# Attention and two mixture layers on one core: where half A's weight parts are loaded, clamped and scaled, and how late the other conversions may stand

## The chip, the cores and the metric

One Trainium2 chip, one core. The metric is the device time of one execution in microseconds (us), the median of the runs shown; lower is better.

## What is computed

Inputs are q, k, v of shape 4 x 8 x 576 x 64 (batch, heads, tokens, width), a threshold tau, and two pairs of float32 weights of 512 x 2048 and 2048 x 512.

```
scores = q @ k^T / 8                            per batch and head
keep   = scores >= max(scores) - tau            else -1e9
attn   = exp(scores - max) / (sum + 1e-9)
x      = attn @ v                               as 2304 x 512
x      = g(x @ w1_in) @ w1_out                  g(h) = h * clip(h + 3, 0, 6) / 6
out    = f(x @ w2_in) @ w2_out                  f(h) = h - tanh(h)
```

The matrix products are made to float32 quality: each operand is split into a high and a low part, and three products (high x high, high x low, low x high) are summed.

## The kernel before

**Order of the work.** The kernel doesn't issue instructions as it is written. It records tasks (`add`, with an engine, an estimated duration, a key, the buffers it reads and writes, and a `slack`), and `Plan.issue` then emits them engine by engine: an engine that is free takes the ready task with the lowest key. `slack` delays the moment at which a task's successors count as ready, so it only moves instructions in each engine's order. On the chip each engine runs its instructions strictly in that order and waits on semaphores. The engines are PE (matmul), DVE, ACT, POOL (GpSimd) and SP, whose queue issues nearly all DMAs.

**Attention.** There are four batches, two column groups each, four pairs of heads. A unit is 128 rows of queries of one head (144 units; `softmax`, L561 on): PE makes 128 x 576 scores in PSUM (L577), DVE takes the maximum (L582), ACT the exponential (L584) and the threshold (L587), DVE masks (L593), ACT and POOL split the result into two float16 parts (L598, L602), and SP transposes it by a DMA (L605) for the products with v (L628). Two PSUM buffers hold scores. Per pair of heads k is transposed and split once (`k_round`, L460 to L485), `LK` units ahead of its first use; v is scaled by a power of two and split (`v_round`: sum of magnitudes on ACT L525, sum over partitions on PE L527, the power on DVE L531 to L536, scaling in place on ACT L539, high part on ACT L541, low part on POOL L543), `LV` units ahead.

**Layer 1, half A.** The hidden width of 2048 is cut in two halves, A and B. For half A layer 1 runs inside the attention stage: after each (batch, group) its tokens go through `layer1` (m tiles L388, gates L691 to L701, second product L734). Half B (`hidden`, `second`) follows after attention, then layer 2 with both halves.

**Weight conversion.** `load_w` (L334) turns a 128-wide part of a weight into a high and a low part, because the values have to pass a bit-level rounding. For each part: a DMA of 512 KB (L350 or L355) into `st`; ACT takes the magnitude of the words (L358); DVE clamps it to a range (L361, the first entry of `steps`), shifts (L363), puts the sign in (L366) and the low bits (L369); ACT writes the high part (L376); POOL subtracts for the low part (L378). There are 16 parts (8 `i`, 8 `o`) for each of: half A and half B of layer 1, half A and half B of layer 2. The working tile is `wu` (SBUF, ring `R_wu` of two); half A of layer 1 passes `scratch=R_m` and works in a PSUM buffer `m` instead, one of the two that `layer1` uses too. The ring `R_st` of three holds the loaded words.

**What sets the places.** Half A's parts are recorded one per unit with the key `T0 + STEP * (W0 + WS * n + ...)` and `slack=ST` (4.0) on the load. `weights(...)` records half B's and layer 2's: `WB` (half B, spacing `WBS`), `Ws[0]` (layer 2, half A, spread over all of half B's stage) and `Ws[1]` (layer 2, half B, from `key - W2B` with spacing `W2S`, while layer 2's first blocks run). In layer 2's first two blocks the gate's low part is on POOL (`low="pool"`, L701), so POOL works there for the gate and for the conversion.

## Time and profile before

| | us |
|---|---|
| median of 3 runs | 1147.84 |
| lowest and highest run | 1145.71, 1150.57 |
| the profiled execution, its own time | 1146.78 |
| its span, first to last instruction | 1144.7 |
| PE busy | 1073.2 (94%) |
| DVE busy | 718.4 (63%) |
| ACT busy | 616.5 (54%) |
| POOL busy | 419.0 (37%) |

The profile is read by stage, not by these averages: the attention stage with half A runs to about 515 us, half B to about 720 us, layer 2 to the end. The 2.1 us between the profiled time and the span lie before the first and after the last instruction.

### The profile page before, as it was taken

To read this page: it belongs to the slowest core of one execution; us is meant where nothing else is said; L and a number is where in the kernel's file an instruction comes from. 1 tells how busy PE (TensorE), PEld (TensorE's weight loads), DVE (VectorE), ACT (ScalarE), POOL (GpSimd) and SP (SyncE) were. 2 spreads that over 40 slices of the span, in tenths; PEclk is the share of its full clock that TensorE was granted. 3 is DMA by queue.
4 is the path that set the end of the run, shared out by engine and by line. 5 is a ranking of instruction groups with operands and counts; after the bars stand their busy time and mean duration, and the time that the engine had idled before them with its cause. 6 is when DMAs were issued, how large, how long until landed. Compare 5 with 4: busy or idle time off the path is not lost.

```text
span 1144.7 us, 23228 instructions
## 1 busy us (share of the span) xinstructions
PE 1073.2 (94%) x9104; PEld 1002.1 (88%) x9104; DVE 718.4 (63%) x1365; ACT 616.5 (54%) x1268; POOL 419.0 (37%) x420
## 2 busy tenths in 40 slices
PE   5668899999999999889999999989999999999998
PEld 4557788998999899889999999978999999999997
DVE  6889887678777867587865663995323333333232
ACT  6868888689677867445544443544323323323222
POOL 3666767667656765652412210465200000000000
PEclk8668899999999999999999999999999999999999
DMA  7889678777977787778633430241100000000000
GB/s 186 180 190 230 131 183 156 173 148 188 164 168 144 167 155 129 210 198 282 184 93 94 129 94 1 76 131 33 38 1 19 1 19 19 1 19 20 1 20 19
DMA packets 257454, 125.77 MB, mean 110 GB/s; under 512 B 200257, under 2 KB 250945, under 8 KB 257345
## 3 DMA queue, kind: packets, MB, share of 16 engines
q1 hardware_dynamic: 247296, 114.72, 43.0%
q0 software_dynamic: 9504, 9.44, 3.6%
q8 instruction: 72, 1.18, 0.4%
q14 instruction: 38, 0.30, 0.1%
q10 hardware_dynamic: 544, 0.13, 0.1%
HBM read 62.92 MB, written 18.87 MB: 71 GB/s over the span
## 4 chain that ended last, share of the span: by engine, by line
PE 74%; DVE 8%; issue 5%; ACT 5%; POOL 3%; DMA 3%; SPq 0%; POOLq 0%; DVEq 0%; ACTq 0%
PE ya L388 24%; PE m L388 18%; PE h L388 12%; PE s L577 7%; PE m L734 6%; PE tp L628 5%; DVE e L593 2%; PE tp L460 2%; POOL bi L378 1%; DVE z L582 1%; ACT e L584 1%; POOL g L701 1%; DMA pt<-pp 1%; DMA st<-in_moe_w_in_dram 1%; DVE st L369 1%
## 5 line engine op out<-in xcount | busy, mean ns | idle before, releaser
L602 POOL TENSOR_TENSOR pp<-e,pp 128x128 f16<-128x128 f32 (+3 forms) x160 | 185.4, 1179 | 119.3 <-ACT pp L598 58.3
L698 ACT ACTIVATE g<-t 128x256 fp32r<-128x256 f32 x216 | 90.0, 417 | 103.8 <-DVE t L905 78.2
L582 DVE TENSOR_REDUCE z<-s 128x1 f32<-128x576 f32 x144 | 108.2, 753 | 53.3 <-PE s L577 52.4
L701 DVE TENSOR_TENSOR g<-t,g 128x256 fp32r<-128x256 f32 x184 | 92.9, 505 | 71.9 <-PE ya L388 44.6
L593 DVE SCALAR_TENSOR_TENSOR e<-s,z,e 128x576 f32<-128x576 f32 x144 | 116.1, 811 | 15.6 <-ACT e L584 9.9
L388 PE MATMUL m<-xT,ai 128*128 128x256 f32 (+1 forms) x768 | 121.7, 304 | 3.7 <-DVE t L693 2.5
L577 PE MATMUL s<-ks,q 128*128 128x288 f32 x512 | 105.2, 334 | 17.2 <-DVE e L593 16.5
L388 PE MATMUL ya<-ao,g 128*128 128x512 f32 x432 | 113.7, 396 | 5.8 <-POOL g L701 4.8
L388 PE MATMUL ya<-g,bo 128*128 128x256 f32 x864 | 116.1, 283 | 2.0 <-DVE g L701 1.9
L584 ACT ACTIVATE e<-s,z 128x576 f32<-128x576 f32 x144 | 105.4, 738 | 23.3 <-DVE z L582 18.3
L388 PE MATMUL h<-x,bi 128*128 128x256 f32 x864 | 115.4, 283 | 0.1
L388 PE MATMUL m<-x,bi 128*128 128x256 f32 x864 | 115.1, 283 | 0.0
L388 PEld LDWEIGHTS h<-x,bi 128*128 128x128 f32 x864 | 111.0, 191 | 3.3 <-POOL bi L378 0.3
L388 PEld LDWEIGHTS m<-x,bi 128*128 128x128 f32 x864 | 111.0, 191 | 3.0
L388 PEld LDWEIGHTS m<-xT,ai 128*128 128x128 f32 x768 | 107.9, 192 | 6.0 <-DVE t L693 3.5
L388 PEld LDWEIGHTS ya<-g,bo 128*128 128x128 f32 x864 | 108.9, 192 | 2.8 <-DVE g L701 2.5
L388 PE MATMUL ya<-bo,g 128*128 128x512 f32 x432 | 111.2, 393 | 0.0
L577 PEld LDWEIGHTS s<-ks,q 128*128 128x128 f32 x512 | 81.7, 210 | 24.4 <-issue 9.3
L628 PE MATMUL tp<-vt,pt 128*128 128x65 f16 (+1 forms) x2240 | 87.9, 199 | 8.1 <-DMA pt<-pp 4.5
L388 PEld LDWEIGHTS ya<-ao,g 128*128 128x128 f32 x432 | 75.9, 189 | 21.1 <-POOL g L701 7.8
L628 PEld LDWEIGHTS <-pt 128*128 128x128 f16 (+1 forms) x2240 | 79.7, 104 | 16.3 <-DMA pt<-pp 6.5
L905 DVE TENSOR_TENSOR t<-h,t 128x256 f32<-128x256 f32 x72 | 30.4, 423 | 98.8 <-ACT t L903 98.8
(101 smaller groups left out, 1825.2 us busy)
## 6 DMA issues: line engine op xcount, KB each, us to landing
st<-in_moe_w_in_dram SPq DMA_DIRECT2D x32, 512.0 KB, 3.9
st<-in_moe_w_out_dram SPq DMA_DIRECT2D x32, 512.0 KB, 4.0
x<-xs POOLq DMA_DIRECT2D x18, 512.0 KB, 5.4
xs<-xT SPq DMA_DIRECT2D x8, 640.0 KB, 4.8
y<-ys SPq DMA_DIRECT2D x9, 512.0 KB, 8.9
kr<-in_k_dram SPq DMA_DIRECT2D x16, 256.0 KB, 3.1
vr<-in_v_dram SPq DMA_DIRECT2D x16, 256.0 KB, 3.6
xs<-xT SPq DMA_DIRECT2D x8, 512.0 KB, 4.5
```

What stands on the lines that cost most here:

```text
L388: nc.tensor.matmul(ps, l[a], r[b], start=first and t == 0 and i == 0, stop=last and t == 2 and i == n - 1,)
L460: nc.tensor.transpose(ps[:, o:o + w], s.rearrange("p r d -> p (r d)"), ident[p0:p0 + w, p0:p0 + w])
L577: nc.tensor.matmul(ps.t[:, half, 0:SH], l, ks[:, half * SH:(half + 1) * SH], start=i == 0, stop=i == len(ops) - 1,)
L582: add("dve", 0.69, key, lambda: nc.vector.tensor_reduce(out=z.t[:, 0:1], in_=s(), axis=AX.XY, op=ALU.max, negate=True), r=[ps], w=[z])
L584: exp = add("act", 0.66, key, lambda: nc.scalar.activation(out=ex(), in_=s(), func=ACTF.Exp, bias=z.t[:, 0:1]), r=[ps, z], w=[e])
L593: add("dve", 0.74, key, lambda: nc.vector.scalar_tensor_tensor(out=ex(), in0=s(), scalar=z.t[:, 1:2], in1=ex(), op0=ALU.is_ge, op1=ALU.mul ...
L602: add("pool", t_pool(w * (src.stop - src.start)), key, lambda src=src, dst=dst: nc.gpsimd.tensor_tensor(out=pp.t[:, 0:w, dst], in0=e.t[:, ...
L628: nc.tensor.matmul(pv.t[0:m, w_ * (D + 1):(w_ + 1) * (D + 1)], pt.t[:, n, blk, rows], vv, start=o == 0, stop=o == len(ops) - 1)
L698: hi = add("act", t_act(n, sbuf=True), key, lambda: nc.scalar.activation(out=gh(), in_=t(), func=ACTF.Copy), r=[bt], w=[bh])
L701: add(low, t_pool(n) if low == "pool" else t_dve(n), key, lambda: eng.tensor_tensor(out=gl(), in0=t(), in1=gh().bitcast(F32), op=ALU.subtr ...
L734: prev = [add("pe", t_mm(n, 1), kd, lambda p=p, l=l, r=r, m=m, s=s, ps=ps: nc.tensor.matmul(ps.t[:, 0:n], W["o", m].t[:, l, s], r[m].t[:, ...
L905: add("dve", t_dve(n), key, lambda: nc.vector.tensor_tensor(out=s_(), in0=p(), in1=s_(), op=ALU.subtract), r=[ps, t], w=[t])
```

## The change

Five things are changed, by numbers of the planner and in `load_w` and `v_round`:

- The first two weight parts of half A are loaded on ACT's queue at the start, with no slack (`queue=n < 2`); the later ones stay on SP's.
- k's first round stands one unit later (`LK` 5 to 4), and the first batch's v rounds stand three units later (`u + 2` for the first pairs in place of `u - LV`).
- v is scaled on POOL in place of ACT.
- In half A's conversion the magnitude is written to `wu` in SBUF, the clamp works there, and only the shift moves on to the PSUM buffer; the first four parts' clamps (`NCL = 4`) are on POOL, the other twelve on DVE. Half B's and layer 2's conversions keep their tile and engine.
- Slacks: `cs` of 0.1 (half B), 0.3 and 0.2 (layer 2) on the tasks of a conversion, three times that on the magnitude; the spacing of layer 2's half B goes from 3.0 to 4.0 (`W2S`).

```diff
-    LK, LQ, LV, LD = 5, 3, 1, 4
+    LK, LQ, LV, LD = 4, 3, 1, 4
+    CB, CC, CD = 0.1, 0.3, 0.2
-    W2B, W2S = 6.0, 3.0
+    W2B, W2S = 6.0, 4.0
+    NCL = 4
...
-        wst, wu, W = R_st.new(), (scratch or R_wu).new(), R_w[name, kind, m].new()
+        wst, wu, W = R_st.new(), R_wu.new(), R_w[name, kind, m].new()
+        sc = scratch.new() if scratch else wu
+        mid = lambda dt: sc.t.bitcast(dt)
+        eng, sync = ("act", nc.scalar) if queue else ("dma", nc.sync)
...
+        def clamp():
+            (nc.gpsimd if low else nc.vector).tensor_scalar(
+                out=part(F32), in0=part(F32), scalar1=TINY, scalar2=HUGE, op0=ALU.max, op1=ALU.min)
...
-            out=part(F32), in_=raw(1).bitcast(F32), func=ACTF.Abs), r=[wst], w=[wu], slack=cs)
+            out=part(F32), in_=raw(1).bitcast(F32), func=ACTF.Abs), r=[wst], w=[wu], slack=3 * cs)
+        if low:
+            add("pool", t_pool(DM), key + 3, clamp, r=[wu], w=[wu], slack=cs)
+        else:
+            add("dve", 0.5, key + 3, clamp, r=[wu], w=[wu], slack=cs)
         steps = [
-            lambda: nc.vector.tensor_scalar(
-                out=part(F32), in0=part(F32), scalar1=TINY, scalar2=HUGE, op0=ALU.max, op1=ALU.min),
             lambda: nc.vector.tensor_scalar(
-                out=part(I32), in0=part(I32), scalar1=3, scalar2=0x3FFFFFF8,
+                out=mid(I32), in0=part(I32), scalar1=3, scalar2=0x3FFFFFF8,
...
-        add("act", t_act(N, sbuf=True, scalars=True), key, lambda: nc.scalar.activation(
-            out=raw(), in_=raw(), func=ACTF.Copy, scale=sv.t[:, 2 * j:2 * j + 1]), r=[vr, sv], w=[vr])
+        add("pool", t_pool(N), key, lambda: nc.gpsimd.tensor_scalar(
+            out=raw(), in0=raw(), scalar1=sv.t[:, 2 * j:2 * j + 1], scalar2=None, op0=ALU.mult), r=[vr, sv], w=[vr])
...
-                rounds.append((u - LV, ("v", b, j)))
+                rounds.append((u + 2 if u < 4 else u - LV, ("v", b, j)))
...
-                    "a", kind, m, ..., 0.8, slack=ST, scratch=R_m, cs=CS)
+                    "a", kind, m, ..., 0.8, slack=ST if n > 1 else 0.0, scratch=R_m, cs=CS, queue=n < 2, low=n < NCL)
```

Line numbers of the changed kernel are 11 higher behind `load_w`; in it the magnitude is L367, the clamp L363, the shift L374.

How the order moves, at three places. First ACT's first instructions (ks: k's split, q: q's split, vt and vr: v, st: loaded words, wu: magnitude, e: exponential). Before:

```order
L449 DMA qr<-in_q_dram 128x2x64 x2
L483 ACT_TABLE_LOAD
L483 ACTIVATE ks<-tp 64x2x256 x2
L490 ACTIVATE q<-tp,tau_b 128x512
L525 ACTIVATE vt_94,vs<-vr 128x10x64
L483 ACTIVATE ks<-tp 64x2x64 x2
L539 ACTIVATE vr<-vr,sv 128x640
L483 ACTIVATE ks<-tp 64x2x256 x2
L541 ACTIVATE vt_94<-vr 128x10x64
L584 ACTIVATE e<-s,z 128x576
```

And with the change:

```order
L460 DMA qr<-in_q_dram 128x2x64 x2
L355 DMA st<-in_moe_w_in_dram 128x4x256 x2
L494 ACT_TABLE_LOAD
L494 ACTIVATE ks<-tp 64x2x256 x2
L501 ACTIVATE q<-tp,tau_b 128x512
L494 ACTIVATE ks<-tp 64x2x64
L367 ACTIVATE wu<-st 128x512
L494 ACTIVATE ks<-tp 64x2x64
L494 ACTIVATE ks<-tp 64x2x256 x2
L595 ACTIVATE e<-s,z 128x576
```

Two weight loads stand ahead of ACT's table load, a magnitude stands where v's first sum stood, and two passes over v are gone from ahead of the first exponential.

Second, DVE at the last masked unit of attention (z: maximum and threshold, e: mask, wu: half B's conversion). Before:

```order
L582 TENSOR_REDUCE z<-s 128x1
L590 TENSOR_SCALAR z<-z,tau_b 128x1
L361 TENSOR_SCALAR wu<-wu 128x512
L363 TENSOR_SCALAR wu<-wu 128x512
L593 SCALAR_TENSOR_TENSOR e<-s,z,e 128x576
L366 SCALAR_TENSOR_TENSOR wu<-st,wu 128x512
```

With the change:

```order
L593 TENSOR_REDUCE z<-s 128x1
L601 TENSOR_SCALAR z<-z,tau_b 128x1
L604 SCALAR_TENSOR_TENSOR e<-s,z,e 128x576
L363 TENSOR_SCALAR wu<-wu 128x512
L374 TENSOR_SCALAR wu<-wu 128x512
```

The last mask now stands ahead of half B's first clamp and shift, no longer behind them.

Third, POOL where layer 2's half B (bi, bo) is converted among the gates' low parts (g); the end of that stretch, of 32 g in all. Before:

```order
L378 TENSOR_TENSOR bi_11357<-st,bi_11357 128x512
L701 TENSOR_TENSOR g<-t,g 128x256
L378 TENSOR_TENSOR bo_11406<-st,bo_11406 128x512
L701 TENSOR_TENSOR g<-t,g 128x256 x2
L378 TENSOR_TENSOR bi_11443<-st,bi_11443 128x512
L701 TENSOR_TENSOR g<-t,g 128x256
L378 TENSOR_TENSOR bo_11475<-st,bo_11475 128x512
L701 TENSOR_TENSOR g<-t,g 128x256 x14
```

With the change:

```order
L389 TENSOR_TENSOR bi_11423<-st,bi_11423 128x512
L712 TENSOR_TENSOR g<-t,g 128x256 x2
L389 TENSOR_TENSOR bo_11475<-st,bo_11475 128x512
L712 TENSOR_TENSOR g<-t,g 128x256
L389 TENSOR_TENSOR bi_11518<-st,bi_11518 128x512
L712 TENSOR_TENSOR g<-t,g 128x256 x2
L389 TENSOR_TENSOR bo_11566<-st,bo_11566 128x512
L712 TENSOR_TENSOR g<-t,g 128x256 x11
```

The 16 parts stood among the first 18 gates and stand among the first 21.

## Rows read from the trace of the kernel before

**Rows 1.** Windows by stage: length, PE, PEld, DVE, ACT, POOL busy us, PE clock, DMA, GB/s.

```profile
7.30:20.00 12.70, 7.38 (x32) 5.96 (x32) 8.80 (x16) 9.45 (x20) 2.09 (x3) 0.91 0.93 254
20.00:96.60 76.60, 53.29 (x431) 44.93 (x431) 68.93 (x116) 59.31 (x113) 50.03 (x45) 0.64 0.86 187
96.60:136.00 39.40, 31.80 (x373) 28.98 (x370) 37.64 (x66) 35.17 (x77) 28.21 (x29) 0.91 0.77 157
136.00:461.00 325.00, 315.57 (x3584) 300.36 (x3582) 247.87 (x484) 254.28 (x487) 212.53 (x216) 0.99 0.80 164
720.00:790.00 70.00, 64.19 (x414) 56.56 (x413) 62.36 (x91) 34.70 (x75) 42.13 (x37) 1.00 0.31 98
```

**Rows 2.** Waits of PE from 0 to 140 us: total us, times, longest us.

```profile
PE s L577 <- DVE e L593: 18.7, 14, 4.9
```

**Rows 3.** DVE's maximum to 130 us: busy us, mean ns, idle before it, releaser.

```profile
L582 DVE TENSOR_REDUCE z<-s 128x1 f32<-128x576 f32 x35 | 26.2, 751 | 5.5 <-PE s L577 5.3
```

**Rows 4.** The clamp's line: lowest, median, highest ns, first and last start.

```profile
L361 DVE TENSOR_SCALAR wu<-wu x48: 408/426/2416, 462.0 to 780.7; 128x512 f32<-128x512 f32 x48
L361 DVE TENSOR_SCALAR m<-m x16: 681/690/700, 23.2 to 127.2; 128x512 f32<-128x512 f32 x16
```

**Rows 5.** POOL's groups to 130 us, columns as in rows 3.

```profile
L602 POOL TENSOR_TENSOR pp<-e,pp 128x1024 f16<-128x1024 f32 x15 | 32.1, 2138 | 0.0
L378 POOL TENSOR_TENSOR ai<-st,ai 128x512 fp32r<-128x512 f32 x8 | 10.4, 1300 | 4.3 <-ACT ai L376 4.3
L543 POOL TENSOR_TENSOR vt<-vr,vt 128x640 f16<-128x640 f32 x4 | 5.4, 1357 | 5.9 <-ACT vt L541 5.9
L453 POOL COPY qr<-qr 128x256 f32<-128x256 f32 x10 | 4.0, 400 | 6.8 <-DMA qr<-in_q_dram 6.8
```

**Rows 6.** Timeline of the start: start us, us, engine, line, what, idle before.

```profile
1.20 0.42 SPq L430 DMA_DIRECT2D kr<-in_k_dram  x1
4.98 1.09 PE L460 MATMUL tp<-ident,kr 128*128 128x128 f32 x4 [4.98 <-DMA kr<-in_k_dram]
6.11 1.19 ACT L483 ACTIVATE ks<-tp 64x512 fp32r<-64x512 f32 x2 [3.08 <-PE tp L460]
8.55 0.47 SPq L350 DMA_DIRECT2D st<-in_moe_w_in_dram  x1
```

**Rows 7.** Windows again: a slice of 20 us at a batch's start.

```profile
280.00:300.00 20.00, 19.12 (x219) 18.04 (x218) 15.62 (x31) 17.20 (x32) 16.92 (x18) 1.00 0.98 166
```

**Rows 8.** Timeline at the end of attention, POOL and DVE.

```profile
459.54 4.63 POOL L602 TENSOR_TENSOR pp<-e,pp 128x1024 f16<-128x1024 f32 x3
462.03 2.42 DVE L361 TENSOR_SCALAR wu<-wu 128x512 f32<-128x512 f32 x1 [0.97 <-ACT wu L358]
464.82 0.81 DVE L593 SCALAR_TENSOR_TENSOR e<-s,z,e 128x576 f32<-128x576 f32 x1
```

**Rows 9.** Waits of PE from 461 to 515 us.

```profile
PE tp L628 <- DMA pt<-pp: 1.6, 2, 1.5
```

**Rows 10.** DVE's groups from 720 to 790 us, columns as in rows 3.

```profile
L366 DVE SCALAR_TENSOR_TENSOR wu<-st,wu 128x512 int32<-128x512 int32 x16 | 19.1, 1191 | 0.2
L369 DVE SCALAR_TENSOR_TENSOR st<-st,wu 128x512 uint32<-128x512 uint32 x16 | 15.2, 948 | 0.2
L361 DVE TENSOR_SCALAR wu<-wu 128x512 f32<-128x512 f32 x15 | 10.3, 685 | 2.1 <-ACT wu L358 2.0
L363 DVE TENSOR_SCALAR wu<-wu 128x512 int32<-128x512 int32 x15 | 9.5, 631 | 0.3
L905 DVE TENSOR_TENSOR t<-m,t 128x256 f32<-128x256 f32 x11 | 4.6, 414 | 2.3 <-ACT t L903 2.3
```

**Rows 11.** Waits of PE from 720 to 790 us, the longest.

```profile
PE ya L388 <- POOL g L701: 4.8, 7, 0.9
```

**Rows 12.** Timeline of PE in layer 2 behind the conversion: two m tiles.

```profile
783.79 1.59 PE L388 MATMUL h<-x,bi 128*128 128x256 f32 x12
786.61 1.59 PE L388 MATMUL m<-x,bi 128*128 128x256 f32 x12
```

More of the change, by code (lines that the diff above doesn't have):

```diff
@@ L331, in attention_moe_moe_kernel, with load_w @@
     w_rings(slot0, "io", "a")
-    def load_w(name, kind, m, src, half, key, step, after=(), slack=0.0, scratch=None, cs=0.0):
-        wst, wu, W = R_st.new(), (scratch or R_wu).new(), R_w[name, kind, m].new()
+    def load_w(name, kind, m, src, half, key, step, after=(), slack=0.0, scratch=None, cs=0.0, queue=None, low=None):
+        wst, wu, W = R_st.new(), R_wu.new(), R_w[name, kind, m].new()
+        sc = scratch.new() if scratch else wu
         f0 = half * FH + m * 128
@@ L354, in load @@
             else:
[L355 to L359 removed]
+                sync.dma_start(out=wst.t, in_=src[f0:f0 + 128, :])
+        def clamp():
+            (nc.gpsimd if low else nc.vector).tensor_scalar(
+                out=part(F32), in0=part(F32), scalar1=TINY, scalar2=HUGE, op0=ALU.max, op1=ALU.min)
+        add(eng, 0.47, key, load, w=[wst], after=after, xfer=1.75, slack=slack)
+        add("act", t_act(DM, sbuf=True), key + 3, lambda: nc.scalar.activation(
+            out=part(F32), in_=raw(1).bitcast(F32), func=ACTF.Abs), r=[wst], w=[wu], slack=3 * cs)
[3 more added lines that the diff above has]
+            add("dve", 0.5, key + 3, clamp, r=[wu], w=[wu], slack=cs)
         steps = [
             lambda: nc.vector.tensor_scalar(
[L362 to L364 removed]
+                out=mid(I32), in0=part(I32), scalar1=3, scalar2=0x3FFFFFF8,
                 op0=ALU.logical_shift_left, op1=ALU.bitwise_and),
             lambda: nc.vector.scalar_tensor_tensor(
[L367 removed]
+                out=mid(I32), in0=raw(1), scalar=-0x40000000, in1=mid(I32),
                 op0=ALU.bitwise_and, op1=ALU.bitwise_or),
             lambda: nc.vector.scalar_tensor_tensor(
[L370 removed]
+                out=raw(1).bitcast(U32), in0=raw(0).bitcast(U32), scalar=29, in1=mid(U32),
                 op0=ALU.logical_shift_right, op1=ALU.bitwise_or),
@@ L373, in load_w @@
         for n, f in enumerate(steps):
-            add("dve", 0.65 if n > 1 or scratch else 0.5, key + 3 + n * step, f,
-                r=[wu] if n < 2 else [wu, wst], w=[wu] if n < 3 else [wst], slack=cs)
+            add("dve", 0.65 if n or scratch else 0.5, key + 3 + (n + 1) * step, f,
+                r=[sc, wu] if n == 0 else [sc, wst], w=[sc] if n < 2 else [wst], slack=cs)
         add("act", t_act(DM, sbuf=True), key + 3 + 4 * step, lambda: nc.scalar.activation(
@@ L812, in attention_moe_moe_kernel @@
                 WA[kind, m] = load_w(
-                    "a", kind, m, w1_in if kind == "i" else w1_out, 0, T0 + STEP * (W0 + WS * n + WO * (kind == "o")), 0.8, slack=ST, scratch=R_m, cs=CS)
+                    "a", kind, m, w1_in if kind == "i" else w1_out, 0, T0 + STEP * (W0 + WS * n + WO * (kind == "o")), 0.8, slack=ST if n > 1 else 0.0, scratch=R_m, cs=CS, queue=n < 2, low=n < NCL)
             if u < NU:
@@ L863, in attention_moe_moe_kernel, with weights @@
         PM = t_mm(NB, 3 * KD)
-        def weights(half, rings_, w_in, w_out, key, step, after=lambda n: ()):
+        def weights(half, rings_, w_in, w_out, key, step, cs, after=lambda n: ()):
             W = {}
@@ L871, in weights @@
                         rings_[kind], kind, m, src, half, key + step * (2 * m + (kind == "o")), 0.8,
-                        after(2 * m + (kind == "o")))
+                        after(2 * m + (kind == "o")), cs=cs)
             return W
@@ L910, in attention_moe_moe_kernel @@
         late = pend[NU - WBU].writers[-1:]
-        WB = weights(1, {"i": "b", "o": "b"}, w1_in, w1_out, start - FW + WBO, WBS, lambda n: late)
+        WB = weights(1, {"i": "b", "o": "b"}, w1_in, w1_out, start - FW + WBO, WBS, CB, lambda n: late)
         key = T2
@@ L951, in attention_moe_moe_kernel @@
         Ws = (
-            weights(0, {"i": "a", "o": "a"}, w2_in, w2_out, T2, (key - T2) / 16, lambda n: [steps[(n * (len(steps) - 16)) // 16]]),
-            weights(1, {"i": "b", "o": "b"}, w2_in, w2_out, key - W2B, W2S, lambda n: [steps[-6]]),
+            weights(0, {"i": "a", "o": "a"}, w2_in, w2_out, T2, (key - T2) / 16, CC, lambda n: [steps[(n * (len(steps) - 16)) // 16]]),
+            weights(1, {"i": "b", "o": "b"}, w2_in, w2_out, key - W2B, W2S, CD, lambda n: [steps[-6]]),
         )
```

6 lines of the change are left out of this document (1 added, 5 removed).

## The prediction

> **What bounds the kernel now.** I began with the windows by stage, because the average (PE 94% busy) hides which engine ends each stage. From 20 to 96.6 us DVE is busy 68.93 of 76.6 us, from there to 136 us 37.64 of 39.4, while PE has 53.29 and 31.80 [rows 1]. The granted clock of PE is 0.64 in the first of these stretches, between its two levels of 1.2 and 2.4 GHz, and 0.91 in the second: PE waits a lot there. The waits name the reason: PE's scores wait 14 times, 18.7 us in all, for DVE's mask, which frees a score buffer [rows 2]. DVE's own idle time to 130 us is mostly the reverse, 5.3 us of waiting for scores [rows 3], so the two hand units to each other with little to spare. DVE sets the start, and what it has to do there beside the softmax is half A's conversion. From 136 to 461 us it is PE: 315.57 of 325 us, DVE 247.87 [rows 1]. From 720 to 790 us PE stands still for 70 - 64.19 = 5.8 us, DVE is busy 62.36 of 70 [rows 1], and PE waits for POOL's low parts of the gate [rows 11], which come late because DVE is full. A microsecond won at the start is kept, as PE's work behind it stays the same.
>
> **Off DVE at the start.** Four clamps go to POOL: 4 x 0.690 us [rows 4] = 2.8 us less on the engine that bounds the stretch. I take all of it. Their price on POOL has no row: POOL has none of this operation. A plain copy of half the size takes 0.400 us, so 0.8 at least, and a subtraction with two inputs of that size 1.300 [rows 5]: 3.2 to 5.2 us for four, on an engine that has 76.6 - 50.03 = 26.6 us free there [rows 1]. They stand behind the magnitude and ahead of DVE's shift, so a part is finished later by this; nobody waits for the first parts before the first m tiles at 96.6 us. At nothing, then; without that cover it is up to 5.2 us.
>
> **Twelve clamps move from PSUM to SBUF.** In PSUM one takes 0.690 us and never leaves 0.681 to 0.700. In SBUF the median is 0.426, but the longest is 2.416 [rows 4]. That one started at 462.03 us, inside three subtractions of POOL that ran from 459.54 for 4.63 us, and ended with them [rows 8]. So in SBUF a clamp is quick alone and can wait out a POOL instruction. Ends: alone, 12 x (0.690 - 0.426) = 3.2 us less; at the mean of 0.685 that the stretch of layer 2 shows [rows 10], where POOL is busy 42.13 of 70 us, nothing; POOL at the start has 50.03 of 76.6, a little more [rows 1]. I take nothing, from the nearest row.
>
> The Trainium skill states this as a rule (page "SBUF — State Buffer", section "Who interferes with whom"): a DVE `tensor_scalar` in a two-port mode and GpSimd hold one shared pair of ports for a whole instruction, and the later one fully blocks. The clamp of 2.416 us agrees. By that rule the upper end can be worked out as an estimate: with POOL's instructions met at random, the rest of one is (15 x 2.138² + 8 x 1.300² + 4 x 1.357² + 10 x 0.400²) / 2 / 130 us = 0.35 us on average, the clamp 0.78, and the sum below 1.0 us worse.
>
> **Earlier weights.** The first weight load was issued at 8.55 us [rows 6], behind k, q and v; now two are issued on ACT's queue behind q. ACT's first work is at 6.11 us, so the two issues and the table load ahead of it are covered. SP's queue loses two issues, so its k, q and v go out sooner, not later. DVE is idle 12.70 - 8.80 = 3.9 us between 7.3 and 20 us [rows 1]; now the first part's three passes, some 0.69 us each, 2.1 in all, can lie there. ACT's order shows its magnitude ahead of the second pair's k, and two passes over v gone from ahead of the first exponential. I take half of it, 1.0 us; ends 0 and 3.9. Against it: 1.05 MB more is under way while the first k is loaded, which lands at 4.98 us and releases PE [rows 6]. At the 254 GB/s of that stretch [rows 1] k's 0.26 MB beside as much of the weights land 1.0 us later; if k waited for both loads, 4.1 us. SP issues k at 1.20 us, ACT the weights behind two loads of q, so most of k's packets are ahead: I take 0.5 us.
>
> **Scaling v on POOL.** ACT loses 16 passes and POOL gains them: 1.0 us each by the copy (0.400 x 640 / 256), 1.357 by the subtraction of this size [rows 5], so 16 to 22 us in all, 12 to 16 of it between 136 and 461 us, where POOL has 112 us free [rows 1]. The later v and k, with `LV` and `LK`, put the same instructions at other places; v's first use is the first product, four units behind the first scores. At nothing; ends 2 us of gain, as ACT delays fewer exponentials, and the loss of the rival below.
>
> **The end of attention.** DVE's last mask stood behind a clamp that was blocked for 2.42 us [rows 8]; in the new order it stands ahead. The split, the transposing DMA and the last products hang on it, and PE waited 1.5 us for that DMA [rows 9]. I take 1.5 us; ends 0 and 3. The slack `CB` moves little else there.
>
> **Layer 2's half B.** A part costs DVE 1.191 + 0.948 + 0.685 + 0.631 = 3.46 us there, a gate 0.414 [rows 10]; a step of PE takes 786.61 - 783.79 = 2.82 us [rows 12]. Sixteen parts stood among 18 gates: 16 x 3.46 / 18 + 0.41 = 3.49 us of DVE per step, 0.67 too much. They stand among 21 now: 3.05 us, 0.23 too much. What is too much falls from 18 x 0.67 = 12.1 us to 21 x 0.23 = 4.8, to 40%; of PE's 5.8 us 2.3 stay, and 3.5 are won. Ends: 1 us if DVE's blocked passes grow with the gates, 5.8 if PE no longer waits.
>
> **Sum:** -2.8 - 1.0 + 0.5 - 1.5 - 3.5 = -8.3 us. On the profiled execution's 1146.78 us (span 1144.7 and 2.1 around it) that is 1138.5. The median of the runs is 1.06 us above it, so 1139.5 us. A measurement of this kernel can tell about 0.5% from no change: 5.7 us, so faster is below 1142.1, slower above 1153.6.
>
> **Rivals.** *Given back.* DVE's saving at the start is eaten by blocked clamps (1.0 us as above), the early part is held by ACT, and layer 2's half B stays as full as it was (1 us won). Then 2.8 - 1.0 + 1.0 + 1.0 = 3.8 us remain: 1144. For it: POOL is busier with the change. Against: the orders differ as planned. 0.28.
>
> *More than that.* Clamps meet POOL seldom (3.2), the idle time at the start is filled (2.9 more), PE waits for nothing in layer 2 (2.3 more): 1139.5 - 8.4 = 1131. 0.08.
>
> *POOL becomes late at each new batch (slower).* POOL runs in order, and v's four scalings stand ahead of the subtractions that the transposing DMAs wait for. At a batch's start POOL is already busy 16.92 of 20 us [rows 7]; 4 x 1.357 = 5.4 us more don't fit in the 3.1 that are free in such a slice. If none of the 5.4 hides, three later batches cost PE 16.3 us: 1156. It decides from 14.1 / 3 = 4.7 us for each batch, the 8.3 won and 5.7 more. Against it: the scalings spread over more than one slice, and a product stands four units behind its scores. 0.09.
>
> *It doesn't do what it says.* The weights on ACT's queue land no earlier, since all loads share the bandwidth, and k is late by the 1.0 us worked out: 8.3 - 1.0 - 0.5 leaves 6.8 if all else holds, so this moves the time to 1141 only; with half of layer 2's gain gone as well 1143. 0.03.
>
> **How the numbers follow.** The forecast has 0.52. Faster is the forecast and "more", 0.60; same is "given back" and the last, 0.31; slower is 0.09. The range of 8 in 10 reaches from 1130, where "more" lies, to 1150: it takes in "given back", a first k late by 4.1 us and part of the loss on POOL, and leaves out most of the slower case.
>
> **What would show it.** Right: the first clamp starts on POOL near 10 us and the first shift on DVE near 12; the first m tile starts 3 to 4 us before 96.6; DVE's clamps in half A have a median near 0.43 and single ones above 1 us; the last mask follows its threshold at once; from 720 us PE's waits for POOL's gate parts fall from 4.8 us to about 2. Wrong: PE waiting for the transposing DMA in the slices at 180, 280 and 380 us; half A's clamps above 1.2 us on average; the first transpose on PE later than 6 us.

## The result, and the profile after

The changed kernel takes **1159.72 us** (median of 4 runs, 1158.38 to 1161.18); the kernel before took 1148.46 in the same session. The ratio is 1.010, 95% interval [1.0074, 1.0125]: **slower by 1.0%**, more than the 0.5% that can be told from no change. The forecast was 1139.5 us, its range 1130 to 1150. The profiled execution took 1158.38 us, its span is 1156.5.

Where it goes is read from when the same PE instruction starts in both traces:

| start of | before, us | after, us | later by |
|---|---|---|---|
| first scores | 10.36 | 10.59 | 0.2 |
| first m tile (layer 1, half A) | 96.60 | 103.75 | 7.2 |
| first m tile of the eighth block | 478.01 | 493.44 | 15.4 |
| half B | 514.15 | 527.69 | 13.5 |
| layer 2 | 722.04 | 738.71 | 16.7 |
| layer 2's half B | 772.99 | 786.02 | 13.0 |
| end of PE's work | 1139.17 | 1151.04 | 11.9 |

So attention lost 15.4 us up to the eighth block, half of it before the first m tile, where 3 to 4 were to be won. Of the two late terms one came: 4.8 us were won from layer 2's start to the end. Another 1.9 were won between the eighth block and half B, but not by the last mask, as the part on the prediction shows. Half B's own stage lost 3.1, which no step of mine had.

The windows up to the first m tile and from there to the eighth block, in the columns of [rows 1], of the kernel before:

```profile
0.00:96.60 96.60, 62.61 (x471) 52.39 (x471) 78.50 (x138) 71.22 (x135) 53.61 (x63) 0.70 0.84 194
96.60:478.01 381.41, 361.34 (x4129) 342.37 (x4125) 297.42 (x569) 296.58 (x580) 248.81 (x251) 0.99 0.79 162
```

and of the kernel after:

```profile
0.00:103.75 103.75, 63.48 (x504) 55.06 (x504) 79.83 (x138) 70.70 (x136) 68.27 (x71) 0.70 0.75 176
103.75:493.44 389.69, 364.79 (x4091) 346.82 (x4089) 295.05 (x564) 288.18 (x564) 271.79 (x264) 0.96 0.77 160
```

To the first m tile DVE is as busy as before (79.83 us against 78.50) although four clamps left it, since three more passes of k's split and one more of the low bits stand ahead of that tile. POOL is 14.7 us busier, and PE has 40.3 us idle in place of 34.0. Behind it PE idles 24.9 us in place of 20.1 and is busy 3.5 longer, at a granted clock of 0.96 in place of 0.99.

What the new passes take, by the tile views of the kernel after (lowest, median, highest ns, first and last start), and DVE's clamps in half A by line (to 140 us, columns of [rows 3]):

```profile
L550 POOL TENSOR_SCALAR vr<-vr,sv x16: 1881/1887/1900, 19.3 to 407.8; 128x640 f32<-128x640 f32 x16
L363 POOL TENSOR_SCALAR wu<-wu x4: 1922/1925/1933, 10.9 to 54.9; 128x512 f32<-128x512 f32 x4
```

```profile
L363 DVE TENSOR_SCALAR wu<-wu 128x512 f32<-128x512 f32 x12 | 9.8, 816 | 1.3 <-ACT wu L367 1.2
```

The scaling takes 1.887 us, where I had 1.0 to 1.357, the clamp 1.925, where I had 0.8 to 1.3. A DVE clamp of half A takes 0.816 us on average and not the 0.690 of PSUM [rows 4].

DVE's and PE's waits from 20 to 104 us, of the kernel before:

```profile
PE s L577 <- DVE e L593: 13.5, 12, 2.6
DVE z L582 <- PE s L577: 2.8, 9, 0.8
```

and after:

```profile
PE s L588 <- DVE e L604: 22.1, 11, 4.1
DVE z L593 <- PE s L588: 9.3, 11, 1.9
```

Both engines wait more for each other: PE for the mask 8.6 us more, DVE for scores 6.5 us more. DVE isn't fuller; the round from scores to mask and back to the scores has become longer.

Most of the 7.2 us arise in one place of DVE's order. The 25th maximum starts 2.6 us later than before, the 26th 7.4. These are passes of DVE between the two, before:

```profile
92.86 0.74 DVE L582 TENSOR_REDUCE z<-s 128x1 f32<-128x576 f32 x1
...
94.06 0.70 DVE L361 TENSOR_SCALAR m<-m 128x512 f32<-128x512 f32 x1 [0.45 <-ACT m L358]
...
95.86 0.81 DVE L593 SCALAR_TENSOR_TENSOR e<-s,z,e 128x576 f32<-128x576 f32 x1
...
97.19 0.75 DVE L582 TENSOR_REDUCE z<-s 128x1 f32<-128x576 f32 x1
```

and after, with a pass of PE (last line) that waits for one of them:

```profile
95.42 0.76 DVE L593 TENSOR_REDUCE z<-s 128x1 f32<-128x576 f32 x1 [0.44 <-PE s L588]
...
97.55 0.54 DVE L363 TENSOR_SCALAR wu<-wu 128x512 f32<-128x512 f32 x1 [0.64 <-ACT wu L367]
...
99.32 0.42 DVE L363 TENSOR_SCALAR wu<-wu 128x512 f32<-128x512 f32 x1
...
102.04 0.68 DVE L692 TENSOR_TENSOR xT<-tp,xT 128x512 fp32r<-128x512 f32 x1
102.64 0.68 DVE L380 SCALAR_TENSOR_TENSOR st<-st,m 128x512 uint32<-128x512 uint32 x1
103.23 0.81 DVE L604 SCALAR_TENSOR_TENSOR e<-s,z,e 128x576 f32<-128x576 f32 x1
...
104.59 0.74 DVE L593 TENSOR_REDUCE z<-s 128x1 f32<-128x576 f32 x1
...
102.77 1.05 PE L639 MATMUL tp<-vt,pt 128*64 128x65 f16 x28 [1.05 <-DVE xT L692]
```

Before, one clamp and one shift stand between the 25th maximum and its mask (95.86). After, all four passes of two weight parts do, from 97.55 to 103.3 us, and the mask waits behind them until 103.23, as does the tokens' low part (`xT`, 102.04), for which PE waits just before the first m tile. That is 4.8 of the 7.2 us.

### The profile page after: what moved, and what is told of

The parts are those of the page before. It is cut to its first block, busy times and chain, and to the rows that moved or that the text cites. A ratio compares the mean times of both kernels' runs of the same rounds, so it can differ in the third digit from the quotient of the medians.

```text
span 1156.5 us, 23229 instructions
## 1 busy us (share of the span) xinstructions
PE 1076.3 (93%) x9104; PEld 1009.4 (87%) x9104; DVE 717.0 (62%) x1361; ACT 605.2 (52%) x1252; POOL 456.1 (39%) x440
## 4 chain that ended last, share of the span: by engine, by line
PE 76%; DVE 11%; ACT 5%; issue 4%; DMA 2%; POOL 2%; SPq 0%; ACTq 0%; DVEq 0%; POOLq 0%
PE ya L399 25%; PE m L399 19%; PE h L399 13%; PE s L588 6%; PE m L745 6%; PE tp L639 5%; DVE e L604 2%; PE tp L471 2%; DVE z L593 2%; DVE ks L496 1%; ACT e L595 1%; ACT pp L609 1%; DVE st L380 1%; DVE wu L377 1%; DMA pt<-pp 1%
## 5 line engine op out<-in xcount | busy, mean ns | idle before, releaser
L588 PE MATMUL s<-ks,q 128*128 128x288 f32 x512 | 108.8, 342 | 24.0 <-DVE e L604 23.0
L588 PEld LDWEIGHTS s<-ks,q 128*128 128x128 f32 x512 | 84.7, 217 | 30.6 <-issue 19.4
L639 PE MATMUL tp<-vt,pt 128*128 128x65 f16 (+1 forms) x2240 | 91.4, 202 | 10.3 <-DVE ks L496 3.2
L639 PEld LDWEIGHTS <-pt 128*128 128x128 f16 (+1 forms) x2240 | 82.5, 106 | 18.5 <-issue 10.5
L609 ACT ACTIVATE pp<-e 128x1152 f16<-128x1152 f32 (+1 forms) x80 | 85.0, 1062 | 10.9 <-DVE e L604 9.5
```

The lines of the kernel that those rows point to most:

```text
L588: nc.tensor.matmul(ps.t[:, half, 0:SH], l, ks[:, half * SH:(half + 1) * SH], start=i == 0, stop=i == len(ops) - 1,)
L609: high = add("act", t_act(w * S, sbuf=True), key, lambda: nc.scalar.activation(out=pp.t[:, 0:w, 0:S], in_=e.t[:, 0:w, :], func=ACTF.Copy), ...
L639: nc.tensor.matmul(pv.t[0:m, w_ * (D + 1):(w_ + 1) * (D + 1)], pt.t[:, n, blk, rows], vv, start=o == 0, stop=o == len(ops) - 1)
```

## The experiments

All runs in one table: the median, the ratio to the kernel before with its interval, and how much later than in the trace of before three points come. The kernel before took 1146.87 to 1148.78 us in the five sessions of these runs, and what a run wins or loses is counted here from the kernel before of its own session. The three points are those of one traced execution, and the executions of one kernel lie 0.7 to 9 us apart: where the two differ, the medians count.

| run | us | ratio [95%] | first m tile | half B | end |
|---|---|---|---|---|---|
| e1_v_on_act | 1153.92 | 1.0050 [1.0032, 1.0068] | 5.2 | 9.8 | 6.4 |
| e2_no_pool_clamp | 1156.75 | 1.0063 [1.0039, 1.0087] | 2.7 | 13.1 | 9.2 |
| e3_no_slack | 1164.59 | 1.0143 [1.0125, 1.0161] | 7.7 | 14.6 | 18.2 |
| e4_k_and_v_as_before | 1151.36 | 1.0026 [1.0015, 1.0037] | 7.3 | 9.8 | 6.0 |
| f1_v_act_k_v_places | 1159.17 | 1.0116 [1.0085, 1.0148] | 4.7 | 13.7 | 9.9 |
| g1_v_scale_64_columns | 1158.47 | 1.0091 [1.0076, 1.0106] | 6.4 | 13.8 | 12.1 |
| g2_clamp_64_columns | 1159.67 | 1.0104 [1.0089, 1.0119] | 7.7 | 16.3 | 14.5 |
| f3_slacks_only | 1146.88 | 0.9994 [0.9984, 1.0005] | 5.0 | 4.6 | 1.2 |
| n1_estimate_scores_054 | 1149.73 | 1.0023 [1.0013, 1.0032] | 0.0 | 0.7 | 2.3 |
| n2_estimate_mask_075 | 1155.22 | 1.0067 [1.0052, 1.0082] | -0.2 | 6.2 | 9.5 |
| p1_measured_prices_in_plan | 1164.78 | 1.0145 [1.0115, 1.0174] | 6.1 | 20.8 | 16.9 |
| h1_slacks_same_attention | 1142.34 | 0.9956 [0.9944, 0.9969] | -0.2 | 0.0 | -3.7 |
| h1c_layer_2_slack_only | 1141.78 | 0.9957 [0.9942, 0.9972] | -0.5 | -1.4 | -5.3 |
| h2_v_on_pool_old_plan | 1159.34 | 1.0103 [1.0088, 1.0119] | 3.9 | 11.2 | 13.9 |
| h4_half_a_clamped_in_sbuf | 1153.12 | 1.0058 [1.0037, 1.0079] | 3.8 | 3.2 | 4.2 |
| h5_half_a_four_clamps_on_pool | 1153.96 | 1.0071 [1.0046, 1.0096] | 3.6 | 3.3 | 6.3 |
| h7_parts_in_old_order | 1161.07 | 1.0110 [1.0093, 1.0128] | 11.2 | 19.0 | 15.1 |
| h6_two_loads_on_act_queue | 1152.27 | 1.0036 [1.0023, 1.0050] | 4.7 | 3.0 | 5.6 |

### One part of the changed kernel undone

e1 gives the scaling of v back to ACT:

```diff
-        add("pool", t_pool(N), key, lambda: nc.gpsimd.tensor_scalar(
-            out=raw(), in0=raw(), scalar1=sv.t[:, 2 * j:2 * j + 1], scalar2=None, op0=ALU.mult), r=[vr, sv], w=[vr])
+        add("act", t_act(N, sbuf=True, scalars=True), key, lambda: nc.scalar.activation(
+            out=raw(), in_=raw(), func=ACTF.Copy, scale=sv.t[:, 2 * j:2 * j + 1]), r=[vr, sv], w=[vr])
```

> The changed kernel with v scaled on ACT again (16 passes); all else as changed. Theory P (GpSimd's own price: its tensor_scalar took 1.89 us for 640 columns where 1.0 to 1.36 had been taken, and POOL works in order ahead of the transposing DMAs): this gives back 3 to 6 us of the 11.3, most of it at the batch starts near 280 and 380 us, so 1154 to 1157. Theory K (k's and v's rounds stand in worse places, and PE waits for k's splits there): no gain, 1158 to 1162.

e2 has all clamps on DVE, e3 no slack (the spacing stays at 4.0), e4 the rounds of k and v at their old places, f1 the edits of e1 and e4 together:

```diff
-    NCL = 4
+    NCL = 0
...
-    CB, CC, CD = 0.1, 0.3, 0.2
+    CB, CC, CD = 0.0, 0.0, 0.0
...
-    LK, LQ, LV, LD = 4, 3, 1, 4
+    LK, LQ, LV, LD = 5, 3, 1, 4
-                rounds.append((u + 2 if u < 4 else u - LV, ("v", b, j)))
+                rounds.append((u - LV, ("v", b, j)))
```

> The changed kernel with the first four clamps on DVE (in SBUF, like the other twelve). Theory P: a clamp on POOL took 1.93 us and stands in order ahead of the softmax's subtractions, so without it the first m tile starts 2 to 5 us earlier than 103.75 us and the time is 1155 to 1158. Theory D (DVE's clamps in SBUF are held up by POOL): four more of them, 1160 to 1163.

> The changed kernel with the three slacks (0.1, 0.3, 0.2) at 0; the spacing of 4.0 stays. Theory S (the slacks moved DVE's passes in half B so that PE waits at 560 us and the clock falls for a moment): half B's stage is 2 to 3 us shorter than 211.0 us, the gain of 4.8 us behind 738 us stays, 1156 to 1158. If the slacks carry layer 2's gain instead, that falls to under 2 us and the time is 1160 to 1163.

> The changed kernel with k's rounds one unit earlier and the first batch's v rounds early again, as before the change. Theory K: PE's waits for k's splits (2.7 + 1.5 us from 136 to 471 us) go, and the time is 1152 to 1156. Theory P: within 2 us of the changed kernel, 1158 to 1162.

> The changed kernel with v scaled on ACT and k's and v's rounds where they were; left are the two loads on ACT's queue, half A's clamps in SBUF with four on POOL, the slacks and the spacing of 4.0. If the two parts cost what they gave back alone (5.8 and 8.4 us) and are independent: 1145 to 1147. If both price the same thing, POOL and ACT being crowded at a batch's start: 1149 to 1152.

The changed kernel is 11.3 us above its kernel before. e1 is 5.1 above, e2 8.0 and e4 2.6, so each wins a part of the loss, e4 most. But e1's 6.1 us and e4's 8.7 don't add up: f1, with both edits, is 11.9 above and wins nothing, outside both of its theories. Nor did e4 win where its theory K had it: from the first m tile to the eighth block PE waits 5.1 us for k's splits in e4, 5.5 in the changed kernel and 0.9 before. An undone part is also a new plan, and these runs alone can't tell a part's price from its order's. (`LK` moves both of k's rounds of every pair of heads, in all four batches, and not only the first, as the list of the change has it.) Only e3 is plain: without the slacks it is 15.8 us above, about 4.5 more than with them, and the gain of layer 2's half B is gone (at its first product the loss is 18.1 us, at the end 18.2). The spacing of 4.0 alone gives nothing, and half B's stage doesn't become shorter (211.3 us): theory S was wrong.

### The same order, a pass cut short

To hold the order fixed I kept every instruction of the changed kernel and made one kind short, first the scaling of v, then the clamps on POOL:

```diff
-            out=raw(), in0=raw(), scalar1=sv.t[:, 2 * j:2 * j + 1], scalar2=None, op0=ALU.mult), r=[vr, sv], w=[vr])
+            out=raw()[:, 0:1, :], in0=raw()[:, 0:1, :], scalar1=sv.t[:, 2 * j:2 * j + 1], scalar2=None, op0=ALU.mult), r=[vr, sv], w=[vr])
...
-                out=part(F32), in0=part(F32), scalar1=TINY, scalar2=HUGE, op0=ALU.max, op1=ALU.min)
+                out=part(F32)[:, 0:64 if low else DM], in0=part(F32)[:, 0:64 if low else DM],
+                scalar1=TINY, scalar2=HUGE, op0=ALU.max, op1=ALU.min)
```

> The changed kernel, instruction for instruction in the same order, but POOL scales 64 of v's 640 columns: the rest of v stays unscaled, so the output is not the reference's. It prices POOL's time for v alone. Theory P: a pass falls from 1.89 to some 0.3 us, and of the 5.8 us that scaling on ACT gave back at least 4 come back: 1153 to 1156. Theory O (the order that comes with POOL's scaling costs, not the pass): under 2 us, 1158 to 1161.

> The changed kernel in the same order, but the four clamps on POOL work on 64 of 512 columns, so some weights stay unclamped. Theory P: the first m tile starts 3 to 5 us before 103.75 us, as a clamp falls from 1.93 to some 0.4 us; time 1155 to 1158. Theory O: first m tile within 1.5 us of 103.75, time 1158 to 1161.

The one is 11.2 us above its kernel before, the other 12.4, the changed kernel 11.3: neither wins. In the changed kernel's own order the length of each of POOL's two new passes is hidden. The loss sits in the order and in what else the order holds; the twelve clamps in SBUF and the early loads were not taken out of it by any run with the order kept.

### The slacks by themselves

f3 is the changed kernel with all but the slacks and the spacing undone; its clamps in PSUM are planned at 0.5 us, not 0.65, so its attention has another order than before:

> The kernel before with nothing but the three slacks and the spacing of 4.0. If layer 2's gain of 4.8 us belongs to them and half B's loss of 3.1 us does not: 1142.5 to 1145. If half B's loss comes with them: 1145.5 to 1148.

h1 puts them into the kernel before, whose order stays as it was up to the last mask of attention:

```diff
+    CB, CC, CD = 0.1, 0.3, 0.2
-    W2B, W2S = 6.0, 3.0
+    W2B, W2S = 6.0, 4.0
...
-            out=part(F32), in_=raw(1).bitcast(F32), func=ACTF.Abs), r=[wst], w=[wu], slack=cs)
+            out=part(F32), in_=raw(1).bitcast(F32), func=ACTF.Abs), r=[wst], w=[wu], slack=3 * cs)
...
```

> The kernel before with the three slacks and the spacing of 4.0 added so that every engine's order up to the last mask of attention stays word for word that of before. Theory O (orders alone decide): the attention stage takes what it took before, layer 2's half B is 4 to 5 us shorter, half B of layer 1 moves by less than 2 us: 1143 to 1146. If half B's loss belongs to the slacks: 1146 to 1148.

f3 comes out even (1146.88): 4.6 us lost by half B, won back in layer 2. As no pass of its attention is new, the 5.0 us that it loses up to the first m tile are its order's. h1 has no such loss and is **faster than both kernels**, 1142.34 us. h1c keeps of the three slacks only `CD`, layer 2's half B:

> The kernel before with the slack of layer 2's half B alone (0.2 us, three times that on the magnitude) and its spacing of 4.0; half B and layer 2's half A have none. If layer 2's half B holds all the gain: 1141 to 1143, layer 2's first half-B tile 5 us earlier against its start, and half B back at its length before (the version with all three slacks lost 1.2 us there). If the other two slacks carry part: 1144 or more.

1141.78 us: that slack, with its spacing of 4.0, carries the gain; without the spacing it wasn't run. h1 and h1c can't be told apart (5.2 and 5.1 us won). From layer 2's start PE finishes 4.8 us sooner in h1c, as in h1 and in the changed kernel. Half B's stage is 0.9 us longer than before in h1c too (-1.4 to -0.5), so that the two other slacks cost 1.2 us there, as I had expected, isn't borne out. The window of [rows 1] for layer 2 and PE's waits in it, of h1c:

```profile
720.00:790.00 70.00, 67.58 (x443) 61.00 (x442) 64.03 (x93) 36.02 (x79) 43.15 (x38) 1.00 0.30 98
```

```profile
PE ya L389 <- POOL g L702: 2.4, 3, 0.9
```

PE stands still for 2.4 us there in place of 5.8, and its wait for POOL's gate parts fell from 4.8 us [rows 11] to 2.4.

### A new order with nothing in it

How much can an order cost that no part asked for? Two kernels are the kernel before with one of the planner's estimates changed by 0.01 us (scores, then DVE's mask); p1 is the changed kernel with the planner's prices of the two POOL passes set to what the profile measured:

```diff
n1
-add("pe", 0.53 * len(hs), key, scores, ...
+add("pe", 0.54 * len(hs), key, scores, ...
n2
-add("dve", 0.74, key, lambda: nc.vector.scalar_tensor_tensor(
+add("dve", 0.75, key, lambda: nc.vector.scalar_tensor_tensor(
p1
-            add("pool", t_pool(DM), key + 3, clamp, ...
+            add("pool", 1.93, key + 3, clamp, ...
-        add("pool", t_pool(N), key, lambda: nc.gpsimd.tensor_scalar(
+        add("pool", 1.89, key, lambda: nc.gpsimd.tensor_scalar(
```

> The kernel before, where the planner takes 0.54 in place of 0.53 us for the scores of a unit and nothing else changes: the same instructions, placed a little otherwise. Theory O (the order before is a lucky one among many near ones, and any new plan of the attention stage loses): 1151 to 1160. Theory P (the changed instructions are the cause): within 2 us of before, 1146.5 to 1150.5.

> The kernel before, where the planner takes 0.75 in place of 0.74 us for DVE's mask: the same instructions, placed a little otherwise. Theory O: 1151 to 1160. Theory P: 1146.5 to 1150.5.

> The changed kernel, and the planner's estimates of GpSimd's two new passes set to what the profile measured: 1.89 us for the scaling (it had 1.48) and 1.93 us for the clamp (it had 1.22). If the loss is a plan made with wrong prices: the attention stage wins 5 us or more of its 15, 1145 to 1153. If the stage's order is as good as random for the time, as the two runs with an estimate changed by 0.01 us had it (+2.3 and +9.5 us): no better than 1154, and anything up to 1164.

By the medians n1 is 2.2 us slower and n2 7.7 (2.3 and 9.5 in the traces), without any change in the work. True prices made the changed kernel no faster, 1164.78 us, 17.9 above its kernel before. So putting these two prices right doesn't bring the loss back; another order alone costs several microseconds, and why these estimates don't tell was not traced.

### The parts in the order of before

The clean question is what each part costs where the order stays. In the next four kernels the planner sees the kernel before (except for h7's slacks, which act only from the end of attention on); only an instruction's engine or place in memory is changed when it is written out. h2 scales v on POOL:

```diff
-        add("act", t_act(N, sbuf=True, scalars=True), key, lambda: nc.scalar.activation(
-            out=raw(), in_=raw(), func=ACTF.Copy, scale=sv.t[:, 2 * j:2 * j + 1]), r=[vr, sv], w=[vr])
+        add("act", t_act(N, sbuf=True, scalars=True), key, lambda: nc.gpsimd.tensor_scalar(
+            out=raw(), in0=raw(), scalar1=sv.t[:, 2 * j:2 * j + 1], scalar2=None, op0=ALU.mult), r=[vr, sv], w=[vr])
```

> The kernel before with its plan kept, and only the instruction that scales v emitted on POOL at the place in the sequence where it stood on ACT; every other engine keeps its order. Theory P: POOL's 1.89 us ahead of its subtractions cost 3 to 8 us, 1151 to 1156. Theory O: within 2.5 us of before, 1146 to 1151.

1159.34 us, 11.8 above its kernel before and more than either theory had, in steps where a batch's v is prepared: +3.9 us by the first m tile, +4.2 from 163 to 185 us (in the time of before), +2.7 from 271 to 292. ACT and POOL of h2 in the second of these, by the timeline (columns as in rows 6):

```profile
166.17 0.74 ACT L584 ACTIVATE e<-s,z 128x576 f32<-128x576 f32 x1
169.40 0.74 ACT L541 ACTIVATE vt<-vr 128x640 f16<-128x640 f32 x1 [2.48 <-POOL vr L539]
...
170.38 0.72 ACT L584 ACTIVATE e<-s,z 128x576 f32<-128x576 f32 x1
...
164.95 2.55 POOL L602 TENSOR_TENSOR pp<-e,pp 128x128 f16<-128x128 f32 x2 [2.94 <-ACT pp L598]
167.46 1.90 POOL L539 TENSOR_SCALAR vr<-vr,sv 128x640 f32<-128x640 f32 x1
...
180.79 1.88 POOL L539 TENSOR_SCALAR vr<-vr,sv 128x640 f32<-128x640 f32 x1 [3.05 <-DVE sv L536]
```

The scaling starts on POOL only behind a split of the softmax, ACT's high part of v waits for it (2.48 us), and the next exponential stands behind the high part in ACT's queue. At 180.79 us it is POOL that stands, 3.05 us for DVE's power of two, with the next splits behind it. Over the whole kernel ACT's wait is, in h2:

```profile
ACT vt L541 <- POOL vr L539: 16.9, 12, 2.6
```

and in the changed kernel:

```profile
ACT vt L552 <- POOL vr L550: 0.2, 1, 0.2
```

So the new order keeps the round trip off ACT, and not by v's later rounds alone: in e4, with the old rounds, this wait is 0.7 us. The time is lost all the same.

h4 writes half A's magnitude and the DVE clamp to the ring in SBUF, with the shift going on into PSUM; h5 also puts the first four clamps on POOL (`wv` is a buffer of the ring in SBUF, `first` a view of it; `low` holds for the first four parts in h5 and for none in h4):

```diff
-            out=part(F32), in_=raw(1).bitcast(F32), func=ACTF.Abs), r=[wst], w=[wu], slack=cs)
+            out=first(F32), in_=raw(1).bitcast(F32), func=ACTF.Abs), r=[wst], w=[wu, wv][:2 if scratch else 1], slack=cs)
...
-            lambda: nc.vector.tensor_scalar(
-                out=part(F32), in0=part(F32), scalar1=TINY, scalar2=HUGE, op0=ALU.max, op1=ALU.min),
+            lambda: (nc.gpsimd if low else nc.vector).tensor_scalar(
+                out=first(F32), in0=first(F32), scalar1=TINY, scalar2=HUGE, op0=ALU.max, op1=ALU.min),
```

> The kernel before with its own plan: each engine's instructions in the same order; only half A's magnitudes, and the DVE clamps of them, go to the ring of half B in SBUF, where the shift moves them on into PSUM (as in the changed kernel). If the attention stage lost its 15 us to the new order alone: 1146 to 1149 us, and the sixteen clamps, which took 0.68 to 1.2 us in PSUM, at 0.41 to 1.0 us. Rival, that DVE's waits for the shared port of SBUF are the loss: 0.4 us more for each of sixteen and what stands behind them, 1152 or more.

> As the run beside it, and the first four of these clamps on GpSimd, in the place in the plan where DVE had them. If a GpSimd pass of 1.9 us costs only where another engine is queued behind it: DVE's shift waits 1.9 us for each, four times in the attention stage; DVE sets the pace in the first 96 us, so up to 4 x (1.9 - 0.7) = +4.8 us at the first tile of the main work, and 1147 to 1153 at the end. If the clamps on GpSimd are hidden as in the run with 64 of their columns: within 1 us of the run beside it.

h4 loses 6.3 us by the median, in its trace 3.8 by the first m tile and 4.2 by the end: the rival. (In PSUM the clamps had taken 0.681 to 0.700 us [rows 4], not up to 1.2.) The cause is in the clamps' rows. DVE's (the first two) and POOL's in one stretch of h4, and all sixteen by line to 140 us:

```profile
60.73 2.35 DVE L367 TENSOR_SCALAR wu<-wu 128x512 f32<-128x512 f32 x1 [0.26 <-ACT wu L364]
64.45 0.42 DVE L367 TENSOR_SCALAR wu<-wu 128x512 f32<-128x512 f32 x1
...
60.28 2.52 POOL L608 TENSOR_TENSOR pp<-e,pp 128x128 f16<-128x128 f32 x2 [0.57 <-issue]
62.74 0.59 POOL L459 COPY qr<-qr 128x256 f32<-128x256 f32 x1
...
L367 DVE TENSOR_SCALAR wu<-wu 128x512 f32<-128x512 f32 x16 | 13.9, 868 | 3.9 <-ACT wu L364 3.8
```

The clamp that starts inside two subtractions of POOL lasts 2.35 us, until just after they are done; the one at 64.45, with POOL idle, takes 0.42. The Trainium skill (page "SBUF — State Buffer", section "Who interferes with whom") has the rule that of a DVE `tensor_scalar` in a two-port mode and a GpSimd instruction the one issued first holds the shared ports for its whole length and the other fully blocks; this clamp agrees. On average a clamp costs 0.868 us and not 0.690: 16 x 0.178 = 2.9 us more on DVE. The other part in the trace is idle: before its clamps DVE waits 3.8 us for ACT's magnitude in h4, 2.6 in the kernel before.

In h5 the four clamps that left DVE are replaced by 3.3 us in which DVE waits for them (half A's shift, to 140 us):

```profile
L369 DVE TENSOR_SCALAR m<-wu 128x512 int32<-128x512 int32 x16 | 10.9, 684 | 3.3 <-POOL wu L367 3.3
```

The first m tile is 0.3 us sooner than in h4 and the end 2.1 later; by medians the two are the same (1153.96 and 1153.12, their intervals overlap). In the changed kernel, where the order is another, no shift waits for POOL: DVE's idle time before the sixteen is 0.2 us.

h7 has all of this at once: h2, h5 and the slacks.

> The kernel before with its own attention order, and in it v scaled on GpSimd, half A clamped in SBUF, its first four clamps on GpSimd, and the three slacks with layer 2's spacing of 4.0; only the two weight loads on ACT's queue and the later rounds of v and k are left out. If the parts' prices in the old order add up (+6.6 for the clamps in SBUF, +1.5 for four of them on GpSimd, +11.9 for v, -5.0 for the slacks, from their medians): +15, 1162 us, so that the parts alone, without any new order, cost what the change costs. If the passes lie beside each other (GpSimd late only once per batch, whatever made it late): 1152 to 1157.

1161.07 us, 12.8 above its kernel before. The expected sum of 15 goes by means; by the medians it is 6.3 + 0.8 + 11.8 - 5.1 = 13.8, so the parts nearly add up: without any new order of attention and without the loads on ACT's queue, they cost about what the change costs (11.3). The steps of h2 stand in it unchanged, +4.1 us from 163 to 185 and +2.7 from 271 to 292, and 11.2 us are lost by the first m tile, more than the 3.9 of v and the 3.6 of the clamps, where they meet in one stretch.

Last, the two early loads alone, in the kernel before, with a new plan:

```diff
-        add("dma", 0.47, key, load, w=[wst], after=after, xfer=1.75, slack=slack)
+        add(eng, 0.47, key, load, w=[wst], after=after, xfer=1.75, slack=slack)
...
-                    "a", kind, m, ..., slack=ST, scratch=R_m, cs=CS)
+                    "a", kind, m, ..., slack=ST if n > 1 else 0.0, scratch=R_m, cs=CS, queue=n < 2)
```

> The kernel before with only the first two weight loads on ACT's queue, without slack, which the change has too; the planner makes a new order from it. If earlier weights are worth what the forecast had (-1.0, ends 0 to -3.9): the first tile of the main work 1 us or more before 96.6 and 1143 to 1147 at the end. If the two transfers take the early transfers of k and q their share of the DMA engines, or the new order costs more than the loads give: the first tile later than 96.6 us, 1148 to 1156.

1152.27 us, 4.0 above its kernel before. The first clamp starts at 10.70 us in place of 23.2 [rows 4], as meant, and the first m tile comes 4.7 us later, not earlier. Whether that is the loads or the new order this run doesn't tell, as both changed.

## Why the prediction was wrong

**What bounds the kernel.** The reading was right that DVE and the scores hand units to each other with little to spare until the first m tile. The step from there failed: "A microsecond won at the start is kept" took DVE's *busy time* for the price and the new order for nothing. What sets the pace is the round from PE's scores over DVE's maximum, ACT's exponential and DVE's mask back to PE, and each engine has other work in its order. Work taken off DVE shortens the round only if what waits for that work isn't late elsewhere, and if nothing else is put ahead of the mask.

**"Off DVE at the start": -2.8.** It came to nothing. DVE lost the clamps but not the time: it idles 23.9 us up to the first m tile in place of 18.1, most of the difference in waiting for scores (9.9 us before its maxima, 5.0 in the kernel before), and the round grew where two weight parts were put ahead of one mask. "Nobody waits for the first parts" holds in the changed kernel (0.2 us before the shifts) and fails in the old order, where the next step of the same part waits, 3.3 us in h5. A clamp took 1.925 us on POOL; that price is hidden in the changed kernel (g2).

**"Scaling v on POOL ... At nothing."** In the old order this step is the dearest: 11.8 us (h2). I looked for room on POOL (112 us free) and never asked who waits for the scaling: ACT's high part, with the exponentials behind it. In the changed kernel's order that wait is gone (0.2 us), and cutting the scaling short wins nothing (g1); the same sentence of the prediction also took "the same instructions at other places" at nothing, and three orders of attention with no new pass in it start the eighth block 3.4 us (n1), 5.0 (f3) and 7.9 (n2) later.

The rival "POOL becomes late at each new batch", 1156 us with a chance of 0.09, came near the time by luck. Its mechanism was that PE waits for the transposing DMA behind POOL. These are PE's waits for it over the whole kernel, of before, of the changed kernel and of h2:

```profile
PE tp L628 <- DMA pt<-pp: 4.5, 4, 2.6
PE tp L639 <- DMA pt<-pp: 1.9, 2, 1.7
PE tp L628 <- DMA pt<-pp: 4.2, 4, 1.8
```

None has grown. h2's steps of 4.2 and 2.7 us at two later batches are of the rival's size, but come through ACT's queue.

**"Twelve clamps move from PSUM to SBUF ... I take nothing."** The mechanism was right and the size too small. The estimate of 0.78 us is near the 0.816 measured; but the upper end of 1.0 us was held to be the sum of longer clamps, and sixteen cost 6.3 us by the median and 4.2 in the trace (h4), 2.9 of it in the clamps themselves. A blocked clamp also holds what stands behind it in DVE's order, the masks for which PE waits among it.

**"Earlier weights": -1.0, +0.5.** The events came as foreseen: the first clamp on POOL at 10.86 us, the first shift at 12.82, k's first transpose 0.7 us later (5.66 against 4.98 [rows 6]). The first mask even ends 1.8 us sooner (16.3 us against 18.1), but the ninth is 1.3 later, and none of the gain reached the first m tile (7.2 us later; 4.7 in h6).

**"The end of attention": -1.5.** This term didn't come. The last mask stands ahead of the clamp, but it waits for ACT's exponential there. In h1, whose order is that of before up to this mask, it starts 0.74 us sooner than at 464.82 [rows 8]:

```profile
464.08 0.82 DVE L594 SCALAR_TENSOR_TENSOR e<-s,z,e 128x576 f32<-128x576 f32 x1 [1.45 <-ACT e L585]
```

PE's wait for the transposing DMA at the end of attention is 1.7 us in the changed kernel, 1.6 before [rows 9]. The 1.9 us between the eighth block and half B (windows of before and after) go with PE's granted clock there, 0.95 in place of 0.91, at which PE is busy 1.5 us less:

```profile
478.01:514.15 36.14, 32.14 (x193) 31.35 (x194) 23.96 (x34) 18.28 (x35) 23.11 (x21) 0.91 0.77 217
493.44:527.69 34.25, 30.60 (x192) 29.82 (x193) 22.95 (x33) 16.94 (x33) 22.29 (x20) 0.95 0.79 222
```

In the five traces with 0.90 to 0.91 there the stretch takes 35.7 to 36.1 us, in the other fifteen, with 0.95 to 1.00, 33.4 to 34.5, wherever the mask stands: n2, with the mask behind the clamp, takes 34.4 and e1, with the mask ahead, 35.9.

**"Layer 2's half B": -3.5.** Right: 3.6 us by the first tile of layer 2's half B and 4.8 by the end. PE's 5.8 us of standing still were to become 2.3 and became 2.4 in h1c. The reason was half right: the slack with the spacing does it, the wider spacing alone does nothing (e3).

**The signs.** Of those named for being right, the first clamp, the first shift, the last mask's place and the waits for POOL's gate parts came; the first m tile did not, nor the clamps' median in half A (0.670 us, not 0.43). Of those named for being wrong none came, and the kernel was slower all the same: no sign was named for a longer round between scores and mask.

**What stays open.** The parts cost 12.8 us in the old order, and the changed kernel loses as much in its own, where POOL's passes are hidden and ACT doesn't wait for them. How much of its loss is the parts and how much the order can't be divided: orders with no new work lost 2.2 and 7.7 us. What the early loads cost with the order kept no run shows. Half B's 3.1 us are 1.8 us of busier PE, at a granted clock of 0.99 in place of 1.00, and 1.4 of waiting:

```profile
514.15:722.04 207.89, 205.77 (x1707) 204.76 (x1706) 136.33 (x260) 92.32 (x193) 42.32 (x38) 1.00 0.42 122
527.69:738.71 211.02, 207.53 (x1707) 206.32 (x1705) 135.67 (x260) 91.63 (x195) 42.74 (x38) 0.99 0.43 121
```

They aren't the change's alone: in the traces of all the runs half B takes 0.9 to 3.4 us longer than in the one trace of before, h2 with no slack among them (2.7).

The best version found is the kernel before with the slack of layer 2's half B and its spacing of 4.0 alone, 1141.78 us, ratio 0.9957 [0.9942, 0.9972].
